# A fused top-k attention and SwiGLU kernel: three turns instead of four from top-k to V, and top-k scratch inside the penalty's buffer

## Chip, core and metric

The kernel runs on one core of a Trainium2 chip. The metric is device time in microseconds (us) of one execution, as the median of the timed runs. All data is FP32.

## What is computed

Attention over 8 batches, 8 heads, 576 tokens, head dimension 64, in which only the 32 largest scores of a row take part; then a SwiGLU block over the 4608 tokens. Cut to what matters:

```python
scores = q @ k.T / sqrt(64)                      # 8 x 8 x 576 x 576
kth    = partition(scores, -32)[..., -32]         # the 32nd largest of a row
scores = where(scores >= kth, scores, -1e9)
attn   = softmax(scores)                          # sum + 1e-9 below
x      = (attn @ v) -> (4608, 512)                # heads side by side
g      = x @ w_gate                               # 512 x 1536
out    = (g * sigmoid(g) * (x @ w_val)) @ w_out   # 1536 x 512
```

## The kernel before

**Units and turns.** The attention is cut into 160 units. A unit is 128 query rows of two heads; each batch has four query tiles (`qt` 0 to 3) by four head pairs, and a fifth tile (`qt == J`, 64 rows) in which the two heads share the 128 partitions, so that its unit has the vector work of one head only. These are called long and short units here. A batch is 16 long units and then 4 short ones.

The main loop makes one turn for each unit `n`. A unit takes part in several turns, each time in another step:

- `scores(n)` (one turn ahead): matmuls into PSUM (L294, L308), copied by ScalarE to a tile `sc` (L299, L313).
- `select(n)`: VectorE finds the 32nd largest value in four rounds of MAX8 (L329), between them MATCH_REPLACE8 (L333), which writes the scores without the eight found. It writes them to a scratch tile `rest`, one buffer. A TENSOR_SCALAR (L339) then writes the penalty, a very negative number where a score is too small and zero elsewhere, to a tile `e`, four buffers.
- `penalize(n)`: GpSimd adds the scores to `e` (L351), and prepares the bias of the softmax (L349).
- `weigh(n)`: ScalarE takes the exponential of `e` in place and sums the rows (L360, L365).
- `normalize(n)`: VectorE takes the reciprocal of the sums (L372), ScalarE multiplies `e` by it (L375).
- `turn(n)`: TensorE transposes `e` into PSUM (`etps`, L387), ScalarE copies it to `et` (L388).
- `values(n)`: TensorE multiplies by V (`av`, L407 and L416), ScalarE copies the result into `xT` (L431), the input of the SwiGLU block.

**Feed-forward blocks.** Every 256 tokens of `xT` are a block. There are 18. A block becomes available when `values` has run for the last unit that touches it. `feed(kb)` yields pieces: 24 gate and value pieces (L471) of one credit each, and then, for all blocks but the first, seven quarter products (L557) of 1.5 credits each. One credit is 8 matmul records of 128x256 in the trace (each matmul leaves two records). The weights are rounded during the first turns by all engines (L106 to L123).

**Order.** The engines run in the order in which the program issues, since a dependency between neighbours is added at the end. So the order inside a turn is the order on every engine's queue. A turn issues, in this sequence: the feed-forward leftovers of ScalarE (`flush(on_act)`); `penalize(n-1)`; the leftovers of GpSimd; `turn(n-3)`; `values(n-4)`; the score matmuls of `n+1`; a weight-rounding step of ScalarE (`early`); `weigh(n-1)`; the score copies of `n+1`; two of seven steps of top-k of `n`; up to two feed-forward pieces; two more steps of top-k; `normalize(n-2)`; transposes of the next K and Q (`fetch`) where they are due; the rest of top-k of `n` and of the pieces.

How many pieces a turn issues comes from `share(n)`: `6.4` credits for a long unit (`7.0` until the last weight tables exist), half of that for a short one, less the attention work of that turn on TensorE. For the last four units every turn issues up to 8.

```python
for m, cost in ((n + 1, 0.7), (n - TURN, 0.6), (n - VALUES, 0.7)):
    if m >= 0:
        others += cost * (0.5 if units[m][1] == J else 1)
```

**Buffers.** PSUM has five banks shared by transposes, scores and values, and three for the feed-forward. In SBUF `sc` has two buffers, `rest` one, `e` four, `et` two.

Of the kernel before, what the change touches and what calls it, by code (L numbers as in the profile page):

```python
# [10 lines left out]
FP32 = mybir.dt.float32  # L11
# [4 lines left out]
P = 128  # L16
TOP_K = 32
LOWEST = -3.4028234663852886e38
# [7 lines left out]
def kernel(  # L26
# [38 lines left out]
    B, H, S, D = q.shape  # L65
# [16 lines left out]
    work = ctx.enter_context(tc.tile_pool(name="work", bufs=2))  # L82
# [118 lines left out]
    def rounding(n):  # L201
        for _ in range(n):
            next(weight, None)
# [70 lines left out]
    def n_heads(qt):  # L274

        return 1 if qt == J else 2

    def scores(n):
        b, qt, hp = units[n]
        slab = preps[b * NHP + hp]  # L280
        sc = work.tile([P, 2 * S], FP32, tag="sc", name="sc", bufs=2)
        halves = [slice(0, D), slice(D, P)]
        half = S // 2

        def bank():
            return ps_t.tile([P, 512], FP32, tag="t", name="s")


        if qt == J:
            banks = [bank() for _ in range(2)]  # L290
            for i, ps in enumerate(banks):
                for d in halves:
                    k0 = R + i * half
                    nc.tensor.matmul(  # L294
                        ps[d, 0:half], slab[d, S + R : S + 2 * R], slab[d, k0 : k0 + half]
                    )
            yield
            for i, ps in enumerate(banks):
                nc.scalar.copy(sc[:, i * half : (i + 1) * half], ps[:, 0:half])  # L299
        else:  # L300
            q0 = S + 2 * R + qt * P
            banks = []
            for i in range(2):
                for hh, d in enumerate(halves):
                    ps = bank()
                    banks.append((i + 2 * hh, ps))
                    k0 = (1 - hh) * R + i * half
                    nc.tensor.matmul(  # L308
                        ps[:, 0:half], slab[d, q0 : q0 + P], slab[d, k0 : k0 + half]
                    )  # L310
            yield
            for i, ps in banks:
                nc.scalar.copy(sc[:, i * half : (i + 1) * half], ps[:, 0:half])  # L313
        state[n] = dict(sc=sc)

    def select(n):

        nh = n_heads(units[n][1])
        sc = state[n]["sc"]
        m = small.tile([P, 2, TOP_K], FP32, tag="m", name="m", bufs=2)  # L320
        heads = [slice(t * S, (t + 1) * S) for t in range(nh)]
        rest = work.tile([P, 2 * S], FP32, tag="rest", name="rest", bufs=1)
        e = work.tile([P, 2 * S], FP32, tag="e", name="e", bufs=4)
        state[n] |= dict(m=m, e=e, heads=heads)
        cur = sc
        rounds = TOP_K // 8
        for r in range(rounds):
            for t, hs in enumerate(heads):
                nc.vector.max(m[:, t, 8 * r : 8 * r + 8], cur[:, hs])  # L329
                yield  # L330
            if r < rounds - 1:
                for t, hs in enumerate(heads):
                    nc.vector.match_replace(  # L333
                        rest[:, hs], m[:, t, 8 * r : 8 * r + 8], cur[:, hs], LOWEST
                    )
                    yield
                cur = rest
        for t, hs in enumerate(heads):
            nc.vector.tensor_scalar(  # L339
                e[:, hs], sc[:, hs], m[:, t, TOP_K - 1 : TOP_K], FAR, ALU.is_lt, ALU.mult  # L340
            )
# [26 lines left out]
    def normalize(n):  # L368
        st = state[n]
        tot, e, heads = st.pop("tot"), st["e"], st.pop("heads")  # L370
        nh = len(heads)
        nc.vector.reciprocal(tot[:, 0:nh], tot[:, 0:nh])  # L372
        yield
        for t, hs in enumerate(heads):
            nc.scalar.mul(e[:, hs], e[:, hs], tot[:, t : t + 1])  # L375

    def turn(n):

        last = units[n][1] == J
        e = state[n].pop("e")  # L380
        et = work.tile([P, 2 * J + 1, P], FP32, tag="et", name="et")
        for c0, cn in ((0, J), (J, 1)) if last else ((0, J), (J, 1), (J + 1, J)):
            ps = ps_t.tile([P, 512], FP32, tag="t", name="etps")
            kl = R if last and c0 == J else P
            for c in range(cn):
                k0 = (c0 + c) * P
                nc.tensor.transpose(ps[0:kl, c * P : (c + 1) * P], e[:, k0 : k0 + kl], ident[:])  # L387
            nc.scalar.copy(  # L388
                et[0:kl, c0 : c0 + cn, :],
                ps[0:kl, 0 : cn * P].rearrange("p (c j) -> p c j", c=cn),  # L390
            )
            if c0 == J:
                yield
        state[n]["et"] = et
# [58 lines left out]
    def flush(queue):  # L453
        while queue:
            queue.pop(0)()
# [201 lines left out]
    NU = len(units)  # L657
# [3 lines left out]
    def piece():  # L661

        if len(on_act) > 1:
            flush(on_act)
        if len(on_pool) > 1:
            flush(on_pool)
        while True:
            if not current:
                if not todo or done.get(todo[0], 0) < NHP * BLK:
                    return 0  # L670
                flush(on_act)
                flush(on_pool)
                current.append(feed(todo.pop(0)))
            cost = next(current[0], 0)
            if cost == 0:
                current.pop()
                continue
            return cost

    def fetch(n):  # L680

        b, qt, hp = units[n]
        i = b * NHP + hp
        if qt == 0:
            yield from prep(i)
        if qt == J and i + NHP < len(pairs):
            load(i + NHP)

    def share(n):


        others = 0.0
# [3 lines that stand above are left out]
        if units[n + 2][1] == 0:  # L696
            others += 0.6

        beside = 6.4 if T[1] else 7.0
        return beside * n_heads(units[n][1]) / 2 - others  # L700

    def pieces(n):
        for _ in range(n):
            if credit[0] >= 1:
                credit[0] -= piece()

    def run(steps):
        for _ in steps:
            pass

    def finish_unit(n):
        values(n)
        b, qt, hp = units[n]
        if qt == J and b + 1 < B:
            load_v((b + 1) * NHP + hp)
# [3 lines left out]
    load(1)  # L719
    run(fetch(0))  # L720
    run(scores(0))
    early[0]()
    run(fetch(1))
    credit = [0.0]
    no = iter(())
    over = {}
    TURN, VALUES = 3, 4
    due = [2.0]
    for n in range(NU + VALUES):
        nh = n_heads(units[n][1]) if n < NU else 1  # L730
        topk = select(n) if n < NU else no
        over[n - 1] = normalize(n - 1) if 0 <= n - 1 < NU else no
        nxt = scores(n + 1) if n + 1 < NU else no
        ahead = fetch(n + 2) if n + 2 < NU else no
        norm = over.pop(n - 2, no)

        def dve(k, beside=True):

            for _ in range(k * nh):
                next(topk, None)  # L740
                due[0] += 5 / 6 if beside else 0
                if due[0] >= 1:
                    due[0] -= 1
                    rounding(1)

        if n >= NU - NHP:
            credit[0] = 8.0
        else:
            credit[0] = min(credit[0] + share(n), share(n) + 1)
        flush(on_act)  # L750
        if 0 <= n - 1 < NU:
            penalize(n - 1)
        flush(on_pool)
        if 0 <= n - TURN < NU:
            run(turn(n - TURN))
        if n >= VALUES:
            finish_unit(n - VALUES)
        next(nxt, None)

        early[0]()  # L760
        if 0 <= n - 1 < NU:
            weigh(n - 1)
        run(nxt)


        dve(2, beside=False)
        if 2 <= n + 2 < NHP:
            load(n + 2)
        if n < NHP:
            load_v(n)  # L770
        pieces(2)
        flush(on_act)
        dve(1)
        dve(1)
        next(norm, None)
        run(norm)

        flush(on_pool)
        next(ahead, None)
        pieces(1)  # L780
        next(ahead, None)
        dve(1)
        pieces(1)
        dve(2, beside=False)
        run(topk)
        pieces(6)
    while piece():
        pass
# [48 lines left out]
```

## Time and profile before

| what | us |
|---|---|
| median of 3 timed runs | 1821.04 (1820.66 to 1822.96) |
| span of the profiled execution | 1817.8 |
| what the median has over the span | 3.2 |
| TensorE busy | 1708.7 |
| VectorE busy | 1610.7 |
| ScalarE busy | 1218.7 |
| GpSimd busy | 1036.4 |

The page gives the profiled execution's span and no other time of its own. Busy time is time in which an engine executes; for TensorE matmuls overlap, so that its busy share says when it had work, not how well it was used. A row of the timeline gives start and duration in us, the engine, the line, the operation, the tiles as output<-inputs, how many instructions were merged, and in brackets how long the engine was idle before, with what released it. The span is also shown as 40 slices of 45.4 us with a digit for the busy tenths of each engine, and with the clock that TensorE was granted.

### The profile page before, as it was taken

The page shows a single profiled execution, that of the slowest core. Times are in us where ns is not written, and L with a number is a line of the kernel's source. Part 1 is how long each engine was busy: PE and PEld are TensorE (multiplying, and loading weights), DVE is VectorE, ACT ScalarE, POOL GpSimd, SP SyncE. Part 2 cuts the span into 40 slices and gives each one's busy share as a digit, 9 for nine tenths or more (in the row PEclk, how much of TensorE's full clock was granted, in tenths as well). Part 3 has the DMA queues.
Part 4 walks back from the last instruction along what each step waited for, and adds up shares of the span by engine and source line. Part 5 has one row for each costly group of instructions (what it writes and reads, how often), then busy time and mean ns, then how long its engine had stood idle before and what let it go on. Part 6 is the DMA issues. An engine that isn't in the chain of part 4 may idle for free.

```text
span 1817.8 us, 30526 instructions
## 1 busy us (share of the span) xinstructions
PE 1708.7 (94%) x10756; PEld 1409.2 (78%) x10756; DVE 1610.7 (89%) x3372; ACT 1218.7 (67%) x2977; POOL 1036.4 (57%) x930
## 2 busy tenths in 40 slices
PE   4458999899999899999999999999999999999999
PEld 2346778687788788887888878887888878888887
DVE  7999999999999799997999989998999989998400
ACT  6778666676667676666767676767676766675532
POOL 5788756455565645554455636564556554646354
PEclk6669999899999999999999999999999999999999
DMA  7432030002100030000300021000300011000000
GB/s 191 125 108 90 14 85 7 12 1 50 45 1 13 2 82 12 13 1 22 73 12 2 13 56 39 1 12 3 74 19 13 1 36 33 1 13 12 1 12 12
DMA packets 109305, 59.65 MB, mean 33 GB/s; under 512 B 88544, under 2 KB 96992, under 8 KB 109152
## 3 DMA queue, kind: packets, MB, share of 16 engines
q1 hardware_dynamic: 108016, 57.37, 12.1%
q8 instruction: 85, 1.39, 0.3%
q14 instruction: 68, 0.56, 0.1%
q10 hardware_dynamic: 1136, 0.33, 0.1%
HBM read 48.23 MB, written 9.44 MB: 32 GB/s over the span
## 4 chain that ended last, share of the span: by engine, by line
PE 86%; DVE 8%; ACT 2%; POOL 2%; issue 2%; DMA 0%; SPq 0%; ACTq 0%; POOLq 0%
PE f L471 41%; PE x_ps L557 9%; PE av L416 8%; PE etps L387 7%; PE s L308 7%; PE y_ps L557 7%; DVE m L329 3%; DVE rest L333 3%; PE s L294 2%; PE av L407 1%; PE o_ps L517 1%; PE kqps L263 1%; DVE size L121 1%; DVE e L339 0%; POOL p L543 0%
## 5 line engine op out<-in xcount | busy, mean ns | idle before, releaser
L329 DVE MAX8 m<-rest 128x8 f32<-128x576 f32 x864 | 612.7, 744 | 2.2
L351 POOL TENSOR_TENSOR e<-e,sc 128x1152 f32<-128x1152 f32 (+1 forms) x160 | 383.1, 2394 | 83.7 <-DVE e L339 76.3
L333 DVE MATCH_REPLACE8 rest<-m,rest 128x576 f32<-128x576 f32 x576 | 423.1, 740 | 0.0
L471 PE MATMUL f<-xT,wg 128*128 128x256 f32 x1728 | 401.6, 382 | 0.0
L471 PE MATMUL f<-xT,wv 128*128 128x256 f32 x1728 | 399.1, 382 | 0.0
L471 PEld LDWEIGHTS f<-xT,wg 128*128 128x128 f32 x1728 | 323.1, 190 | 62.6 <-issue 21.3
L471 PEld LDWEIGHTS f<-xT,wv 128*128 128x128 f32 x1728 | 324.5, 190 | 58.7 <-issue 16.6
L499 POOL TENSOR_TENSOR h<-h,half_g 128x512 f32<-128x512 f32 x108 | 138.2, 1280 | 292.7 <-ACT h L498 292.2
L329 DVE MAX8 m<-sc 128x8 f32<-128x576 f32 x288 | 205.0, 747 | 104.0 <-ACT sc L299 57.8
L388 ACT COPY et<-etps 128x512 f32<-128x512 f32 (+1 forms) x448 | 184.1, 483 | 131.0 <-PE etps L387 130.2
L360 ACT ACTIVATE e<-e,bias 128x576 f32<-128x576 f32 x288 | 222.1, 777 | 57.5 <-POOL e L351 57.2
L387 PE MATMUL etps<-ident,e 128*128 128x128 f32 (+1 forms) x1312 | 184.5, 286 | 79.3 <-POOL size L122 18.2
L504 POOL TENSOR_TENSOR h<-h,val 128x512 f32<-128x512 f32 x108 | 139.6, 1293 | 186.3 <-ACT val L503 186.1
L387 PEld LDWEIGHTS etps<-ident,e 128*128 128x128 f32 (+1 forms) x1312 | 159.6, 147 | 106.0 <-POOL size L122 20.7
L375 ACT ACTIVATE e<-e,tot 128x576 f32<-128x576 f32 x288 | 212.0, 790 | 0.9 <-DVE tot L372 0.9
L333 DVE MATCH_REPLACE8 rest<-m,sc 128x576 f32<-128x576 f32 x288 | 211.5, 740 | 0.0
L308 PE MATMUL s<-kqT 64*128 64x288 f32 x1024 | 178.8, 449 | 14.1 <-ACT kqT L268 8.3
L339 DVE TENSOR_SCALAR e<-sc,m 128x576 f32<-128x576 f32 x288 | 177.2, 651 | 3.4
L416 PE MATMUL av<-et,v 128*64 128x128 f32 (+1 forms) x2560 | 170.3, 278 | 0.0
L313 ACT COPY sc<-s 128x288 f32<-128x288 f32 x512 | 164.0, 402 | 2.9 <-PE s L308 2.9
L496 ACT ACTIVATE h<-f 128x512 f32<-128x512 f32 x108 | 65.2, 604 | 133.3 <-PE f L471 133.3
L416 PEld LDWEIGHTS av<-et,v 128*64 128x64 f32 x2560 | 134.1, 143 | 22.8 <-issue 6.8
(73 smaller groups left out, 2029.1 us busy)
## 6 DMA issues: line engine op xcount, KB each, us to landing
v<-in_v_dram SPq DMA_DIRECT2D x32, 256.0 KB, 2.9
kq_in<-in_k_dram SPq DMA_DIRECT2D x63, 128.0 KB, 2.8
kq_in<-in_q_dram SPq DMA_DIRECT2D x63, 128.0 KB, 3.0
w<-in_moe_w_gate_dram SPq DMA_DIRECT2D x12, 512.0 KB, 3.7
w<-in_moe_w_val_dram SPq DMA_DIRECT2D x12, 512.0 KB, 3.8
w<-in_moe_w_out_dram SPq DMA_DIRECT2D x12, 512.0 KB, 3.5
out_dram<-o SPq DMA_DIRECT2D x38, 128.0 KB, 2.4
out_dram<-o SPq DMA_DIRECT2D x16, 256.0 KB, 2.4
```

What stands on the lines that cost most here:

```text
L308: nc.tensor.matmul(ps[:, 0:half], slab[d, q0 : q0 + P], slab[d, k0 : k0 + half])
L329: nc.vector.max(m[:, t, 8 * r : 8 * r + 8], cur[:, hs])
L333: nc.vector.match_replace(rest[:, hs], m[:, t, 8 * r : 8 * r + 8], cur[:, hs], LOWEST)
L339: nc.vector.tensor_scalar(e[:, hs], sc[:, hs], m[:, t, TOP_K - 1 : TOP_K], FAR, ALU.is_lt, ALU.mult)
L351: nc.gpsimd.tensor_tensor(e[:, every], e[:, every], sc[:, every], ALU.add)
L360: nc.scalar.activation(e[:, hs], e[:, hs], AF.Exp, bias=bias[:, t : t + 1], scale=scale, accum_out=tot[:, t : t + 1],)
L375: nc.scalar.mul(e[:, hs], e[:, hs], tot[:, t : t + 1])
L387: nc.tensor.transpose(ps[0:kl, c * P : (c + 1) * P], e[:, k0 : k0 + kl], ident[:])
L388: nc.scalar.copy(et[0:kl, c0 : c0 + cn, :], ps[0:kl, 0 : cn * P].rearrange("p (c j) -> p c j", c=cn),)
L416: nc.tensor.matmul(av[hh * R : (hh + 1) * R, 0:ql], v_last[:, hh, :] if c == J else vt[:, hh, c, :], moving, start=last and c == 0, stop=c ...
L471: nc.tensor.matmul(ps[:, i, :], w[:, kc, m * P : (m + 1) * P], x[:, kc, :], start=(kc == 0), stop=(kc == KC - 1),)
L557: nc.tensor.matmul(ps, lhsT, T[i][m], start=m == 0, stop=m == MQ - 1)
```

## The change

The step after top-k is shortened by one turn. `normalize(n-1)` has its reciprocal at the end of turn `n`, behind all of top-k, and its two multiplications at the start of turn `n+1`, ahead of `values` and the scores. `turn` comes in the middle of a turn, for the unit two back, where normalization was. `values` is for the unit three back. The score copies are issued right after the score matmuls, ahead of `weigh`. MATCH_REPLACE8 writes to `e`, which the penalty overwrites later, so that `rest` is gone; `e` has three buffers and `sc` three.

```diff
     def scores(n):
...
-        sc = work.tile([P, 2 * S], FP32, tag="sc", name="sc", bufs=2)
+        sc = work.tile([P, 2 * S], FP32, tag="sc", name="sc", bufs=3)
...
     def select(n):
...
-        rest = work.tile([P, 2 * S], FP32, tag="rest", name="rest", bufs=1)
-        e = work.tile([P, 2 * S], FP32, tag="e", name="e", bufs=4)
+        e = work.tile([P, 2 * S], FP32, tag="e", name="e", bufs=3)
...
                     nc.vector.match_replace(
-                        rest[:, hs], m[:, t, 8 * r : 8 * r + 8], cur[:, hs], LOWEST
+                        e[:, hs], m[:, t, 8 * r : 8 * r + 8], cur[:, hs], LOWEST
                     )
                     yield
-                cur = rest
+                cur = e
...
-    over = {}
-    TURN, VALUES = 3, 4
+    scaled = no
+    TURN, VALUES = 2, 3
...
     for n in range(NU + VALUES):
...
-        over[n - 1] = normalize(n - 1) if 0 <= n - 1 < NU else no
+        norm = normalize(n - 1) if 0 <= n - 1 < NU else no
...
-        norm = over.pop(n - 2, no)
...
         if 0 <= n - 1 < NU:
             penalize(n - 1)
         flush(on_pool)
-        if 0 <= n - TURN < NU:
-            run(turn(n - TURN))
+        run(scaled)
         if n >= VALUES:
             finish_unit(n - VALUES)
-        next(nxt, None)
-
+        run(nxt)
         early[0]()
         if 0 <= n - 1 < NU:
             weigh(n - 1)
-        run(nxt)
...
         flush(on_act)
         dve(1)
         dve(1)
-        next(norm, None)
-        run(norm)
+        if 0 <= n - TURN < NU:
+            run(turn(n - TURN))
...
         run(topk)
+        next(norm, None)
+        scaled = norm
         pieces(6)
```

## The prediction

> **What bounds the kernel now.** I read the 40 slices first, to see which engine is full where; then TensorE's timeline at the start; then TensorE's waits; then the timeline of the end. The slices:
>
> ```profile
> PE   4458999899999899999999999999999999999999
> DVE  7999999999999799997999989998999989998400
> PEclk6669999899999999999999999999999999999999
> ```
>
> VectorE is full from the first slices and done before the last two. TensorE is half idle in three and a half slices, at a reduced clock, and full to the end. So this is VectorE-bound for some 150 us and TensorE-bound after it. Only removing TensorE idle time shortens the span. All of it is 1817.8 - 1708.7 = 109 us; a table of 40 us windows puts 77 of that before 160 us, 8.2 in the window 320 to 360, the rest in crumbs of 1 to 5. The start, in TensorE's timeline:
>
> ```profile
> 130.80 2.15 PE L387 MATMUL etps<-ident,e 128*128 128x128 f32 x9 [4.84 <-POOL size L122]
> ...
> 143.61 2.15 PE L387 MATMUL etps<-ident,e 128*128 128x128 f32 x9 [7.08 <-POOL wo L123]
> ...
> 149.20 1.39 PE L308 MATMUL s<-kqT 64*128 64x288 f32 x6 [0.56 <-ACT et L388]
> 150.52 3.72 PE L471 MATMUL f<-xT,wg 128*128 128x256 f32 x16
> 154.08 3.62 PE L471 MATMUL f<-xT,wv 128*128 128x256 f32 x16
> 157.53 3.62 PE L471 MATMUL f<-xT,wg 128*128 128x256 f32 x16
> 160.98 1.15 PE L387 MATMUL etps<-ident,e 128*128 128x128 f32 x9
> ```
>
> The transposes open a turn. Turn 10 starts at 130.80, turn 11 at 143.61. Turn 10 ends in 7.08 us of nothing; in turn 11 the first block is available (units 0 to 7, the last at `values(n-4)`), and the 48 records, six credits, run to the next turn: 10.46 us, 1.74 a credit. The waits of TensorE from 160 to 1700 us (total, times, longest):
>
> ```profile
> PE etps L387 <- issue: 12.4, 8, 3.6
> PE etps L387 <- ACT e L375: 9.9, 7, 4.6
> ```
>
> Of these 22.3 us, 8.2 lie at 338 to 356, where blocks 0 and 1 are used up and block 2 isn't there until turn 31 (its first matmul is at 361.11): three turns of attention alone. The other 14 are at short units. VectorE's own waits there (`m` for `sc`, 72 us from 160 to 1675) cost nothing while TensorE is full. The end:
>
> ```profile
> 1746.53 2.75 PE L557 MATMUL x_ps<-wo,h 128*128 128x256 f32 x12
> ...
> 1751.69 0.77 PE L387 MATMUL etps<-ident,e 128*128 128x128 f32 x5 [0.99 <-ACT e L375]
> ...
> 1754.14 3.72 PE L471 MATMUL f<-xT,wg 128*128 128x256 f32 x16
> ```
>
> Block 16 ends at 1749.3, the last block starts at 1754.1 and fills TensorE to the end; only 1 us there is idle.
>
> **What the skill says.** "Perfetto Trace Analysis", Optimization Strategy: where the most contended engine changes over time, interleaving the regimes may help. The slices show just two such regimes. "TensorE: Matmul & The Clock Gate", What's actually happening: after idling the array runs at half clock until it has been busy for a few us; the nine transposes take 2.15 us at the start and 1.15 at 160.98, which agrees. "SBUF — State Buffer", Who interferes with whom: a TENSOR_SCALAR in a two-port mode and GpSimd block each other, an instruction with one SBUF input outside these modes doesn't. L339 has a median of 510 ns and a maximum of 2035, MAX8 727 to 762, which fits. So a changed phase between the two engines moves only L339.
>
> **The change part by part.**
>
> Scratch in `e`: 864 MATCH_REPLACE8 stay at 740 ns, and the SBUF is 4.6 KB a partition smaller. New is a wait: the first MATCH_REPLACE8 of unit n must wait for the transposes of n-3, in the middle of turn n-1. A TensorE-bound turn lasts 11.37 us (transposes at 321.60 and 332.97); in it the transposes would follow 1.5 us of `av`, 1.2 of scores and two pieces, 3.5, and end at 7.4. VectorE begins a turn 6.6 us or more after TensorE began the turn before (802.51 to 809.08), and its first replacement 1.4 later, at 8.0. It just misses the wait. Behind it would stand all of top-k, and GpSimd's L351 after that; bounds: 0 to 1 us of VectorE a turn, none of it on the path where TensorE is full. I take 0.
>
> Score copies ahead of `weigh`: four copies of 0.4 us no longer stand behind L351 (2.4 us) and two exponentials. VectorE's wait for `sc` should shrink. But the reciprocal at the end of top-k of n now waits for `weigh(n-1)`, and the next top-k is queued behind it. That is the same chain (L339, L351, L360, L365), less the copies (1.28 us) and plus, on ScalarE, the multiplications (1.5 us) that run while GpSimd adds. VectorE's lead stays within about 1 us of what it was: 0.
>
> The reciprocal itself leaves the middle of the next top-k, half a turn earlier: a gain where TensorE waited for the multiplications behind it (12.4 us of "issue", of which 4.8 outside the hungry turns). What is late next is `et`: `av` at the head of turn n+1 needs copies that stand on ScalarE behind `weigh` and the gate functions, as the multiplications did before. So most of the 7.9 us of the second row stays. Bounds for all crumbs: 14 us gained to 17 lost (34 waits of L360 for L351 by half a us each). I take 2 gained.
>
> `values` a turn earlier: block 0 starts in turn 10. Its six credits fall into the 7.08 us that were idle, and everything after follows a turn earlier. All 36 weight pieces get two steps each, five steps a turn: by turn 10 some 54 steps, 25 pieces ready; the block wants 24 within five turns. Nothing to wait for. While VectorE sets the pace, up to turn 30, this changes no turn's time. At the hungry turns block 2 starts in turn 30 (347.4) instead of 31 (356.1); the hunger is as long as before. From there the lead is one long turn's pieces: 6.4 - 0.7 - 0.6 - 0.7 = 4.4 credits, 4.4 x 1.74 = **7.6 us** of TensorE work done in idle time, which the tail no longer has. V's loads on SP are issued a turn earlier, from turn 19, in a queue that is then nearly empty: 0. DVE may lose up to 1 us in turn 10, by L339 beside more GpSimd work: 0 to 2, I take 0.5.
>
> The end: block 16 now ends inside turn 159, and the last unit's chain lies open: the last copy of the block 0.6, multiplication 0.8, `xT` copy 0.2, exponential with sums 1.3, reciprocal 0.2, multiplication 0.8, transposes 0.7, copy 0.7, `av` 1.0: 6.3 us against the 4.9 seen, so 1.4 lost (0, if ScalarE is ahead, to 4, if GpSimd's L351 is late).
>
> Sum: -7.6 - 2 + 0.5 + 1.4 = -7.7. Span 1810; with the 3.2 us that the median has over the span, **1813**.
>
> **The rivals.** Main case, the lead carried to the end: 0.56; its own range is 1808 to 1818.
> *More*: looser coupling also removes the 14 us of crumbs. For it: reciprocal and copies both come earlier. Against: `et` takes the multiplications' place. 1821 - 7.6 + 0.9 + 1.4 - 12 = 1804, chance 0.16.
> *Nothing*: the lead is given back, since blocks come as they are used up and the last chain is open, or waits on `e` and `et` keep V as late as it was. The price is 4 us at the end and 3 in hungry turns: 1820, chance 0.14.
> *Slower*: `av` at the head of a turn waits for `et`. With the numbers above, the copies end at 9 to 10 us of 11.4 when L351 is on time; in the turn from 624.63 the exponential came at 632.01, 7.4 us in, and with 2.1 for it, 1.8 for gate functions and 1.2 for the copies they end at 12.6, 1.2 too late. If the 34 turns in which L360 waits for L351 cost 0.5 us each, that is 17 us: 1830. It decides from 0.23 us a turn on (7.7 / 34). For it: GpSimd is 57% busy and in order. Against: transposes had the same queue ahead of them before. 0.14.
>
> **How the numbers follow.** About 0.2%, 3.6 us, is what a measurement can tell here. Faster takes the whole of "more" and nearly all of the main case: 0.70. Same takes "nothing" and the main case's edge: 0.16; slower 0.14. The range, 1803 to 1823, leaves out the slower case and some of "more".
>
> **What would show it.** Right: the first L471 near 138, a turn of 12 us before 150.5; the first of block 2 near 350; the last block's start 4 to 8 us before 1754; idle time of TensorE before 160 us about 8 lower; the clock up one slice earlier. VectorE's waits for `sc` should shrink, with waits of L372 for L365 in their place, and few for L387. Wrong: a row of `av` waiting for L388 of over 8 us, or a first L471 at 138 with the last block no earlier.

## The result and the profile after

The changed kernel takes **1809.38 us** (median of 4 runs, 1809.13 to 1810.53) against 1820.98 for the kernel before (4 runs on the same chip). The ratio is 0.9936, with a 95% interval of 0.9922 to 0.995: 11.6 us faster, where 8 were forecast. The profiled execution took 1810.53 us with a span of 1808.5. The spans differ by 9.3 us. The other 2.3 come from the two executions that were profiled. In the 67 runs of the kernel before beside the experiments, the time is 1.7 to 1.9 us longer than the span, and 2.0 in those of the change. So the 3.2 us by which the median before exceeds its profiled span mean that this execution was some 1.4 us shorter than usual; the one after was 1.1 us longer than its median.

Line numbers of the changed kernel are lower by one from the top-k on: L470 is a gate or value matmul, L386 a transpose, L387 the `et` copy, L406 and L415 are `av`. The slices of its page:

```profile
PE   4559999799999999999999999999999999999999
DVE  7999999999999999998999989998999979999400
PEclk7559999999999999999999999999999999999989
```

TensorE gains in the second and fourth slice, and it has a 7 instead of an 8 in the eighth, where the hungry turns are (turns for which no feed-forward block is available). New is the 8 in its clock in the last slice but one. TensorE's timeline at the start, and at block 2:

```profile
130.91 0.80 PE L406 MATMUL av<-et,vlast 128*128 128x128 f32 x2 [3.12 <-ACT et L387]
...
135.66 3.75 PE L470 MATMUL f<-xT,wg 128*128 128x256 f32 x16
139.25 1.15 PE L386 MATMUL etps<-ident,e 128*128 128x128 f32 x9
...
147.14 0.38 PE L406 MATMUL av<-et,vlast 128*128 128x128 f32 x2
...
347.44 1.56 PE L470 MATMUL f<-xT,wg 128*128 128x256 f32 x6
```

The first gate records stand at 135.66 instead of 150.52, and the transposes now come between them. Block 2 begins at 347.44 instead of 361.11. TensorE's idle time before 160 us fell from 77.5 to 66.7. But there is a wait that was not there before, in brackets in the first row: `av` waits for `et`. TensorE's waits from 160 to 1700 us (total, times, longest):

```profile
PE av L406 <- ACT et L387: 17.6, 19, 2.7
PE av L415 <- ACT et L387: 3.2, 5, 0.6
```

and VectorE's over the whole run:

```profile
DVE tot L371 <- ACT tot L364: 79.7, 32, 14.4
...
DVE e L332 <- PE etps L386: 25.2, 29, 2.3
DVE m L328 <- ACT sc L313: 9.3, 1, 9.3
```

The waits of MAX8 for `sc` (57.8 us for L299 and 46.1 for L313 before) have all but gone, and the reciprocal waits for the sums instead. MATCH_REPLACE8 does wait for the transposes that free its buffer. The end, in the timeline of all engines:

```profile
1730.41 2.75 PE L556 MATMUL x_ps<-wo,h 128*128 128x256 f32 x12
...
1733.92 1.27 POOL L542 TENSOR_TENSOR o<-o,p 128x512 f32<-128x512 f32 x1 [1.83 <-ACT o L645]
1735.33 1.40 POOL L350 TENSOR_TENSOR e<-e,sc 128x576 f32<-128x576 f32 x1
1736.76 0.78 ACT L359 ACTIVATE e<-e,bias 128x576 f32<-128x576 f32 x1 [2.20 <-POOL e L350]
...
1743.20 5.38 PE L470 MATMUL f<-xT,wg 128*128 128x256 f32 x16
```

Block 16 ends at 1733.2, 16 us earlier than before, but the last block starts only 10.9 us earlier. Between the two lie 10.0 us instead of 4.9: GpSimd adds the last unit's scores (L350) after block 16's last sum (L542), and everything of that unit follows. TensorE idles in it, and the first 16 records of the last block then take 5.38 us instead of 3.72.

**A balance.** TensorE runs in the program's order, so its time can be cut at the first score record of units 20, 140 and 159. "Rest" is the time of a stretch less 0.2158 us for each feed-forward record in it (16 records at full speed stand 3.45 us apart; a record of block 0's output counts as two). It holds attention, waits, and what a lower clock costs; the last column ends with TensorE's last record. All numbers are worked out from one trace of each kernel; "six batches" is units 20 to 139, split into the five units that open a batch, the ten long ones after them, and the last five, of which four are short. Three pairs of kernels that hardly differ (before and the scratch of experiment 1; the change and seven credits; V late with three `et` buffers and with two) agree within 1.4 us until unit 20 and within 0.8 in six batches.

| kernel | unit 20 at, with records done | rest of six batches: opening / long / short | sum | rest, last batch | rest after unit 159 |
|---|---|---|---|---|---|
| before | 235.4, 248 | 113.2 / 230.7 / 129.0 | 472.9 | 74.3 | 10.1 |
| after | 233.9, 288 | 117.0 / 228.3 / 127.4 | 472.8 | 70.0 | 15.5 |
| copies first (four turns) | 235.2, 248 | 112.5 / 233.9 / 131.6 | 478.0 | 73.0 | 10.1 |
| normalize first only | 239.1, 248 | 124.2 / 253.3 / 122.5 | 500.0 | 77.2 | 9.1 |
| copies behind, V late | 235.2, 248 | 121.1 / 246.8 / 116.6 | 484.5 | 71.8 | 9.6 |
| V late | 229.8, 248 | 111.1 / 233.3 / 112.2 | 456.6 | 70.7 | 9.6 |
| V late, two `et` | 231.2, 248 | 111.1 / 232.5 / 112.2 | 455.8 | 70.7 | 9.6 |
| transposes at head | 238.2, 288 | 116.6 / 243.9 / 113.6 | 474.1 | 72.7 | 13.3 |
| transposes before gates | 236.3, 288 | 124.0 / 230.0 / 126.8 | 480.8 | 71.5 | 17.6 |
| V in mid-turn | 235.5, 288 | 120.3 / 239.4 / 123.3 | 483.0 | 72.3 | 18.0 |
| seven credits | 233.7, 288 | 117.0 / 228.3 / 127.5 | 472.8 | 70.0 | 9.0 |
| transposes by kind | 234.1, 288 | 117.0 / 228.3 / 111.8 | 457.1 | 69.7 | 8.9 |

From before to after: 1.5 us less until unit 20, which is hardly more than two traces differ by, and 40 records more done by then (8.6 us), together -10.1; nothing in six batches; -4.4 in the last batch; +5.4 after unit 159. That is the 9.3 us, within rounding. The experiments ask what the nothing in six batches is made of, and whether the rest of the sum is what I took it for.

### The profile page after: what moved, and what is told of

The parts are those of the page before. It is cut to its first block, busy times and chain, and to the rows that moved or that the text cites. A ratio compares the mean times of both kernels' runs of the same rounds, so it can differ in the third digit from the quotient of the medians.

```text
span 1808.5 us, 30379 instructions
## 1 busy us (share of the span) xinstructions
PE 1703.6 (94%) x10756; PEld 1402.5 (78%) x10756; DVE 1615.7 (89%) x3372; ACT 1221.0 (68%) x2977; POOL 1039.2 (57%) x930
## 3 DMA queue, kind: packets, MB, share of 16 engines
q8 instruction: 85, 1.39, 0.3%
## 4 chain that ended last, share of the span: by engine, by line
PE 83%; DVE 8%; ACT 6%; POOL 2%; issue 0%; DMA 0%; SPq 0%; ACTq 0%; POOLq 0%
PE f L470 40%; PE x_ps L556 9%; PE av L415 8%; PE s L308 7%; PE y_ps L556 7%; PE etps L386 6%; DVE m L328 3%; DVE e L332 3%; PE s L294 2%; PE av L406 2%; ACT et L387 1%; PE o_ps L516 1%; ACT e L359 1%; DVE e L338 1%; DVE size L121 1%; ACT kqT L268 1%
## 5 line engine op out<-in xcount | busy, mean ns | idle before, releaser
L328 DVE MAX8 m<-e 128x8 f32<-128x576 f32 x864 | 614.1, 746 | 3.3
L350 POOL TENSOR_TENSOR e<-e,sc 128x1152 f32<-128x1152 f32 (+1 forms) x160 | 383.0, 2394 | 86.1 <-DVE tot L371 70.1
L332 DVE MATCH_REPLACE8 e<-m,e 128x576 f32<-128x576 f32 x576 | 423.1, 740 | 0.0
L470 PE MATMUL f<-xT,wg 128*128 128x256 f32 x1728 | 406.5, 383 | 0.6 <-ACT xT L430 0.6
L470 PE MATMUL f<-xT,wv 128*128 128x256 f32 x1728 | 403.4, 382 | 0.0
L470 PEld LDWEIGHTS f<-xT,wg 128*128 128x128 f32 x1728 | 321.6, 191 | 61.0 <-issue 19.8
L470 PEld LDWEIGHTS f<-xT,wv 128*128 128x128 f32 x1728 | 320.6, 190 | 59.3 <-issue 19.7
L387 ACT COPY et<-etps 128x512 f32<-128x512 f32 (+1 forms) x448 | 182.4, 480 | 53.6 <-PE etps L386 52.8
L332 DVE MATCH_REPLACE8 e<-m,sc 128x576 f32<-128x576 f32 x288 | 211.5, 739 | 0.0
L386 PE MATMUL etps<-ident,e 128*128 128x128 f32 (+1 forms) x1312 | 175.9, 279 | 18.7 <-ACT xT L430 12.7
L386 PEld LDWEIGHTS etps<-ident,e 128*128 128x128 f32 (+1 forms) x1312 | 155.9, 144 | 42.7 <-issue 25.2
L313 ACT COPY sc<-s 128x288 f32<-128x288 f32 x512 | 167.6, 417 | 26.5 <-PE s L308 25.3
L308 PE MATMUL s<-kqT 64*128 64x288 f32 x1024 | 170.3, 454 | 15.9 <-ACT kqT L268 15.1
L415 PE MATMUL av<-et,v 128*64 128x128 f32 (+1 forms) x2560 | 173.6, 280 | 6.9 <-ACT et L387 6.9
L415 PEld LDWEIGHTS av<-et,v 128*64 128x64 f32 x2560 | 136.4, 144 | 32.1 <-ACT et L387 9.3
```

What stands on the lines that cost most here:

```text
L308: nc.tensor.matmul(ps[:, 0:half], slab[d, q0 : q0 + P], slab[d, k0 : k0 + half])
L332: nc.vector.match_replace(e[:, hs], m[:, t, 8 * r : 8 * r + 8], cur[:, hs], LOWEST)
L350: nc.gpsimd.tensor_tensor(e[:, every], e[:, every], sc[:, every], ALU.add)
L387: nc.scalar.copy(et[0:kl, c0 : c0 + cn, :], ps[0:kl, 0 : cn * P].rearrange("p (c j) -> p c j", c=cn),)
L415: nc.tensor.matmul(av[hh * R : (hh + 1) * R, 0:ql], v_last[:, hh, :] if c == J else vt[:, hh, c, :], moving, start=last and c == 0, stop=c ...
L470: nc.tensor.matmul(ps[:, i, :], w[:, kc, m * P : (m + 1) * P], x[:, kc, :], start=(kc == 0), stop=(kc == KC - 1),)
```

## The experiments

Each kernel ran beside the kernel before; the ratio is to that, with its 95% interval.

**1. Scratch in `e`, alone and taken back.** Alone, in the kernel before:

```diff
-        rest = work.tile([P, 2 * S], FP32, tag="rest", name="rest", bufs=1)
...
-                        rest[:, hs], m[:, t, 8 * r : 8 * r + 8], cur[:, hs], LOWEST
+                        e[:, hs], m[:, t, 8 * r : 8 * r + 8], cur[:, hs], LOWEST
...
-                cur = rest
+                cur = e
```

> The kernel before with one part: MATCH_REPLACE8 writes to e (four buffers kept), rest is gone. The prediction took 0 for it: 1820 to 1822 us, MATCH_REPLACE8 at 740 ns. Rival: a MATCH_REPLACE8 that waits for transposes of an older unit costs VectorE time in the VectorE-bound start and lengthens the span, over 1823.

Measured: 1820.95 us, 1.0003 (0.9995 to 1.0012). Taken back in the changed kernel (a separate `rest`, `e` still with three buffers):

> The changed kernel with MATCH_REPLACE8 writing to a tile of its own again (one buffer), e with three and sc with three buffers. VectorE's waits of MATCH_REPLACE8 for transposes (25 us in 29 waits) go. The prediction's value for this wait was 0, since VectorE has slack where TensorE is full: 1807.5 to 1811. Rival (VectorE's lead is what TensorE lives on at short units, so the waits are on the path): 1795 to 1805.

Measured: 1808.94 us, 0.9936 (0.9924 to 0.9949), the ratio of the change itself. The 25.2 us of waits at MATCH_REPLACE8 are gone from its profile, and VectorE's waits at the reciprocal have grown from 79.7 to 98.9 us instead. Most of the waiting has moved elsewhere. The scratch costs nothing that can be measured here, as forecast.

**2. The score copies ahead of `weigh`, in four turns.** The kernel of experiment 1 (scratch in `e`, four buffers), with three `sc` buffers and:

```diff
-        next(nxt, None)
-
+        run(nxt)
         early[0]()
         if 0 <= n - 1 < NU:
             weigh(n - 1)
-        run(nxt)
```

> The kernel before, with MATCH_REPLACE8 writing to e (four buffers kept), three buffers of sc, and the score copies issued ahead of weigh; normalization in mid-turn, transposes at the head, four turns, as before. In the changed kernel TensorE reaches the scores of unit 159 at 1706.3 us instead of 1714.1, 7.8 us earlier, beside the feed-forward lead. Theory A (the early score copies free VectorE from GpSimd and ScalarE): these 7.8 us appear here too, 1812 to 1816 us, and the waits of m for sc (104 us before) nearly vanish. Theory B (the reciprocal at the end of top-k, ahead of a turn instead of inside it, does it): VectorE's waits shrink, but TensorE gains nothing, 1819.5 to 1822.5.

Measured: 1825.16 us, 1.0022 (1.0014 to 1.003). Both theories missed. VectorE's waits for `sc` fell only from 104 to 89 us, and TensorE's rest rose by 5 in six batches. In the old order this part loses. The third `sc` buffer and the new place of the copies come together here; no run has them apart.

**3. Normalization at the head of a turn, with the old order behind it.** The changed kernel, four `e` buffers, and:

```diff
-    TURN, VALUES = 2, 3
+    TURN, VALUES = 3, 4
...
         run(scaled)
+        if 0 <= n - TURN < NU:
+            run(turn(n - TURN))
...
         dve(1)
-        if 0 <= n - TURN < NU:
-            run(turn(n - TURN))
```

> The changed kernel with transposes for unit n-3 back at the head of the turn, values four units back, e with four buffers; normalization first, score copies first and scratch in e stay. It stands beside the version with values four units back (1793.9 us), from which it differs only in where the transposes stand. Theory H1 (the gain of that version comes from transposes in mid-turn: TensorE has V, scores and two pieces to do before it needs e, and runs ahead in the VectorE-bound start): 1814 to 1821. Theory H2 (it comes from the reciprocal ahead of the turn instead of inside it, so that nothing waits for the multiplications): 1791 to 1800, and no waits of etps after 400 us.

Measured: 1853.68 us, 1.0186 (1.0172 to 1.02), slower than both theories. That is 59 us more than V late with two `et` buffers (1794.93, experiment 5), which has its transposes in mid-turn instead of at the head of the next turn, and three `e` buffers, and differs in nothing else. The first row of TensorE's waits after 160 us:

```profile
PE s L308 <- ACT et L387: 27.7, 26, 6.0
```

The scores wait for `et` copies, which they don't read. Scores, transposes and `av` share five PSUM banks, and a bank that transposes filled comes free with its copy. On ScalarE that copy now stands behind the two multiplications (1.5 us). A long turn asks for eight banks in the order three for transposes, one for `av`, four for scores. If the five are given in turn, the second, third and fourth of the score matmuls take the banks of the same turn's transposes. The idle time fits that: in the first 15 units of each of the six batches, 177 ns on average stand ahead of the second score matmul and 70 ahead of the third, none ahead of the first. The wait shown is the smaller part. Idle time after 160 us is 38.3 us instead of 31.5, but TensorE's busy time rose from 1708.7 to 1734.7 us for the same 10756 matmul records.

**4. The other half of that pair.** The changed kernel with V a turn later, three `et` buffers, and the score copies behind `weigh` as before:

```diff
-    TURN, VALUES = 2, 3
+    TURN, VALUES = 2, 4
...
-        run(nxt)
+        next(nxt, None)
         early[0]()
         if 0 <= n - 1 < NU:
             weigh(n - 1)
+        run(nxt)
```

> The version with values four units back (1793.9 us), with the score copies behind weigh again as in the kernel before. Theory (the copies ahead of weigh give VectorE its scores without GpSimd; since VectorE now waits at its reciprocal for the same weigh, they matter little): 1793 to 1797. Rival (the copies ahead are worth what VectorE waited for sc before, some of it on the path): 1800 to 1812.

Measured: 1826.14 us, 1.003 (1.0019 to 1.0041), 32 us slower than the same kernel with the copies ahead (experiment 5) and beyond what the rival gave it. TensorE's waits after 160 us:

```profile
PE etps L386 <- ACT sc L313: 26.2, 15, 4.2
```

The transposes don't read `sc`; what they can need of a score copy is the bank that it frees. So with transposes in mid-turn the copies have to stand ahead of `weigh`. Experiments 2 to 4 together: copies first, without the other two parts, +5 us; with normalization moved too, but not the transposes, +33; both moved, but not the copies, +6. The parts gain only together. The rows of waits point to the order in which ScalarE frees PSUM banks as what couples them; no run with another number of banks tests that.

**5. V as late as before.** The changed kernel with `values` four back and three `et` buffers:

```diff
-        et = work.tile([P, 2 * J + 1, P], FP32, tag="et", name="et")
+        et = work.tile([P, 2 * J + 1, P], FP32, tag="et", name="et", bufs=3)
...
-    TURN, VALUES = 2, 3
+    TURN, VALUES = 2, 4
```

> The changed kernel with values again four units back (et gets a third buffer), all else as changed: blocks become available a turn later. Theory: of the 11.6 us gained, the feed-forward lead (4.4 credits, 7.6 us) is lost, and the open chain ahead of the last block (10.0 us from the end of block 16 to the first matmul of block 17, 4.9 before; 1.7 more at a reduced clock) is covered again: 1809.4 + 7.6 - 6.9, so 1808 to 1813. Rival 1 (the lead is all of the gain): 1819 to 1822. Rival 2 (the chain stays open a turn later): 1815 to 1818.

Measured: **1793.91 us**, 0.9855 (0.9838 to 0.9871). No theory had that: 15.5 us faster than the change, though blocks start a turn later again (first gate record at 145.40) and 248 records are done at unit 20 instead of 288. It reaches unit 20 at 229.8, 4.1 us sooner than the change, so that the early V is ahead there by 4.5 us and not by the whole 8.6. The rest of six batches is 16.2 lower, and nearly all of that lies at the short units (127.4 to 112.2). A pair of short turns in TensorE's timeline of the change, then one of this kernel:

```profile
838.43 1.15 PE L386 MATMUL etps<-ident,e 128*128 128x128 f32 x9
840.93 0.49 PE L406 MATMUL av<-et,vlast 128*128 128x128 f32 x2 [1.35 <-ACT et L387]
```

```profile
834.80 1.15 PE L386 MATMUL etps<-ident,e 128*128 128x128 f32 x9
835.78 0.39 PE L406 MATMUL av<-et,vlast 128*128 128x128 f32 x2
837.12 1.19 PE L294 MATMUL s<-kqT 64*64 64x288 f32 x8
```

In the change, `av` follows right behind the transposes whose copies it needs, and TensorE stands still. Here it reads copies of the turn before and starts at once. From scores to scores the same work (16 gate or value records, nine transposes, `av`) takes 8.67 us in the change (833.76 to 842.43) and 7.00 here (830.12 to 837.12). The third buffer isn't needed:

```diff
-    TURN, VALUES = 2, 3
+    TURN, VALUES = 2, 4
```

> The changed kernel with one number changed: VALUES is 4 instead of 3; et keeps its two buffers. The version with three buffers took 1793.9 us. Theory (what counts is the half turn between the copies to et and av; a unit's et is written in the middle of turn n, after av of the unit two before has read that buffer at its head): 1793 to 1797. Rival (the third buffer is needed, the copies to et wait for av): 1799 to 1808.

Measured: 1794.93 us, 0.9855 (0.9841 to 0.987). So the later V alone does it. Unit 20 comes at 231.2 here, and the early V is ahead by 5.9 us.

**6. What `et` stands behind.** Three ways to have `et` earlier with V kept early. First, the transposes ahead of the mid-turn gate functions of ScalarE:

```diff
         pieces(2)
+        if 0 <= n - TURN < NU:
+            run(turn(n - TURN))
         flush(on_act)
         dve(1)
         dve(1)
-        if 0 <= n - TURN < NU:
-            run(turn(n - TURN))
```

> The changed kernel with the transposes of unit n-2 and their copies issued ahead of the mid-turn flush of ScalarE's leftovers, so that the copies to et no longer stand behind gate functions (1.8 us a gate); the order on TensorE and VectorE stays. Theory (values three units back makes av wait for et at the head of the next turn, 17 us in rows of av after 160 us, and this is what the version with values four units back gets rid of): these waits fall by half or more, 1799 to 1806 us. Rival (the waits come from TensorE's own transposes or from the exponential, or cost nothing, and the version with values four units back gains by the order of blocks alone): 1808 to 1811.

Measured: 1820.96 us, 0.9999 (0.9991 to 1.0007): the whole gain lost, half of it at the openings of batches (117.0 to 124.0), and the short units hardly better (126.8). TensorE's waits of `av` at these short units fell only from 10.5 us in 13 cases to 8.0 in 12, so gate functions ahead of the copies aren't the main cause of them. A short turn without any shows what is left:

```profile
847.27 1.15 PE L386 MATMUL etps<-ident,e 128*128 128x128 f32 x9
848.60 0.29 ACT L364 ACTIVATE tot<-tot,eps 128x1 f32<-128x1 f32 x1
848.80 1.22 ACT L387 COPY et<-etps 128x512 f32<-128x512 f32 x3
849.59 0.49 PE L406 MATMUL av<-et,vlast 128*128 128x128 f32 x2 [1.18 <-ACT et L387]
```

The copies follow the last step of `weigh` and take 1.22 us, and TensorE has nothing else to do meanwhile. ScalarE's waits for transposes rose from 52.8 us in 57 cases to 137.9 in 110: the gate functions now stand behind copies that wait for TensorE. Second, the transposes right behind the scores, ahead of `weigh`:

```diff
         run(nxt)
+        if 0 <= n - TURN < NU:
+            run(turn(n - TURN))
         early[0]()
...
         dve(1)
-        if 0 <= n - TURN < NU:
-            run(turn(n - TURN))
```

> The changed kernel with the transposes of n-2 and their copies issued right behind the scores, ahead of weigh on ScalarE; values stays three units back. Outside the feed-forward records, TensorE's time from the scores of unit 20 to those of unit 140 is 473 us in the changed kernel and 457 with values four units back, nearly all of the difference in the short units. Theory (the copies to et stand behind weigh, and av at the head of the next turn waits for them; in a short turn nothing is left to cover that): the short units lose their waits and the lead of a turn stays, 1790 to 1801 us. Rival (transposes now come before TensorE has feed-forward pieces to do, so that they wait for the multiplications at the head): the waits move from av to etps, 1808 to 1825.

Measured: 1817.67 us, 0.9979 (0.997 to 0.9989). Theory and rival were both there: the short units fell to 113.6, with hardly a wait of `av` left, but the long ones rose from 228.3 to 243.9. TensorE's waits after 160 us:

```profile
PE etps L386 <- ACT xT L430: 15.5, 19, 2.6
...
PE av L406 <- ACT et L387: 0.6, 1, 0.6
```

The pieces that stood ahead of the transposes, and covered the multiplications and `xT` copies on ScalarE, now come after them. Third, `values` moved to mid-turn, just ahead of the transposes:

```diff
-        if n >= VALUES:
-            finish_unit(n - VALUES)
...
         dve(1)
+        if n >= VALUES:
+            finish_unit(n - VALUES)
         if 0 <= n - TURN < NU:
```

> The changed kernel with values(n-3) moved from the head to the middle of the turn, just ahead of the transposes of n-2: av gets half a turn of slack for et, and a block still becomes available a turn earlier than with values four units back. Theory (the waits of av for et cost 16 us from unit 20 to 140 and part of the 5.4 us at the end, the lead is worth 4.5 us against the version with values four units back): 1789 to 1797. Rival (what is gained from values four units back is the time of the blocks, not the wait of av; or the banks of PSUM, taken in another order, bring a wait of their own): 1800 to 1812.

Measured: 1827.39 us, 1.004 (1.0028 to 1.0053). The waits of `av` are gone but for 3.8 us at the end; scores now wait for `kqT` and `xT` copies (25.5 and 16.7 us over the whole run), long units cost 239.4, and TensorE is busy 1734.9 us with the same matmul records. That the order of banks is behind it fits experiments 3 and 4, but no run here isolates it.

**7. The last turns.** The change with seven credits instead of eight in the last four turns and the drain:

```diff
         if n >= NU - NHP:
-            credit[0] = 8.0
+            credit[0] = 7.0
```

> The changed kernel with 7 credits instead of 8 in each of the last four turns and the drain, so that some four pieces of block 16 are left for the turns in which the last unit runs through softmax, transposes and V. Theory (an open chain of 5.2 us and a cold clock of 1.7 us were paid there): 1803 to 1806, block 17 starts 4 to 6 us earlier. Rival (the last unit itself comes later by what is left out, or the chain hangs on GpSimd's last sums whatever is issued): 1808 to 1811.

Measured: 1802.95 us, 0.9906 (0.9891 to 0.9921). The rest after unit 159 falls from 15.5 to 9.0, and the last block starts at 1738.13. With eight credits block 16 is used up while the last unit still has its chain to go; with seven, two credits of it (16 records: 704 to 688 in the last batch, 384 to 400 behind it) are kept to cover that chain.

**8. The parts that gained, together.** V early, the transposes at the head only in the turns that select a short unit and in the drain, seven credits:

```diff
         run(nxt)
+        at_head = n >= NU or units[n][1] == J
+        if at_head and 0 <= n - TURN < NU:
+            run(turn(n - TURN))
...
-        if 0 <= n - TURN < NU:
+        if not at_head and 0 <= n - TURN < NU:
```

> The changed kernel (values a turn early kept), with the transposes and et copies at the head of the turn, behind the scores and ahead of weigh, only where the unit in selection is a short one or the stream is draining; in the turns of long units they stay mid-turn; and 7 credits instead of 8 at the last four turns. Theory (the changed kernel's short turns wait for et copies that stand behind weigh and the gates, its long turns do not, and its tail is 6 us of two extra pieces): the short turns lose some 14 us of rest over six batches (127.4 to 113), the tail 6, the lead stays, long units stay at 228: 1785 to 1796 us. Rival (what decides is the order in which PSUM banks are asked for over several turns; switching the place twice a batch has long and short turns wait for each other's banks): 1798 to 1812 us, with the long units' rest above 233 or the batch starts above 121.

Measured: **1788.09 us**, 0.9821 (0.9807 to 0.9834), the fastest of all. Its terms are those of the parts: short units 111.8, long ones unchanged at 228.3, 8.9 after unit 159, 288 records at unit 20. A short turn in ScalarE's timeline, then the same turn and the start of the last block in TensorE's:

```profile
830.76 1.24 ACT L387 COPY et<-etps 128x512 f32<-128x512 f32 x3 [0.18 <-PE etps L386]
831.87 0.80 ACT L359 ACTIVATE e<-e,bias 128x576 f32<-128x576 f32 x1
```

```profile
830.07 1.20 PE L386 MATMUL etps<-ident,e 128*128 128x128 f32 x9
831.10 3.62 PE L470 MATMUL f<-xT,wg 128*128 128x256 f32 x16
834.56 0.38 PE L406 MATMUL av<-et,vlast 128*128 128x128 f32 x2
...
1721.56 0.69 PE L415 MATMUL av<-et,v 128*64 128x64 f32 x16 [0.57 <-ACT et L387]
...
1722.44 3.72 PE L470 MATMUL f<-xT,wg 128*128 128x256 f32 x16
```

The copies now stand ahead of `weigh`, and 16 gate records cover them. Against V late with two `et` buffers, 40 more records are done at unit 20 (8.6 us) which comes 2.9 us later, six batches cost 1.3 more, and the two last stretches 1.7 less: 6.1 us less by the balance, 6.8 by the medians.

## Why the prediction came out as it did

The forecast, 1813 with a main case of 1808 to 1818, holds the 1809.4 measured, and its leading term is part of what happened. That the sum came this near is in part luck: terms that it left at or near nothing came out large and cancelled.

**The lead: there, but not alone.** Forecast 7.6 us; measured at unit 20: 40 records more (8.6 us), reached 1.5 us sooner, 10.1 in all. The first block did start in turn 10, with its first record at 135.66 where I put it near 138, and block 2 at 347.44, the time worked out for turn 30. But V late, whose blocks start as late as those of before, also reaches unit 20 sooner than before, by 4.2 to 5.6 us with the same 248 records (231.2 and 229.8 instead of 235.4). So about half of the 10.1 comes from the new order of the other stages while VectorE sets the pace, where I took 0. The early V adds 4.5 to 5.9 to that (experiment 5), and 5.7 in experiment 8: less than forecast. Which part of the order helps at the start is open; experiments 2 to 4 have none of the gain (235.2, 239.1, 235.2). The idle time before 160 us fell by 10.8, not 8, but with V late it falls by 6.9 to 7.9 too (69.6 and 70.6 us instead of 77.5), so that this sign of being right couldn't tell the two apart. The clock did not come up a slice earlier.

**The crumbs: right in sum, wrong in parts.** I took -2; it came to about nothing in six batches and -4.4 in the last one. The step that failed is the bracket "14 us gained to 17 lost", in which I treated *more* and *slower* as two cases of which one would hold. Both came true at once, and that they cancel is luck.

With V late (experiment 5) the new order of normalization, score copies and transposes is worth 17.1 us over six batches (472.9 to 455.8), 16.8 of it at the short units: that is *more*, and larger than the 12 I gave it. There 9.9 us are idle time that went (11.9 to 2.0); the rest lies inside busy time.

With V early, 17.0 is given back (455.8 to 472.8), 15.2 of it at the short units. There 10.5 us are rows of `av` waiting for `et`, and the rest shows as no wait. With the transposes moved ahead of `weigh` there, `av` waits no more at these units and they fall to 113.6 and 111.8 (experiments 6 and 8): that is the wait of *slower*. That its price was 17 too is chance, since it was worked out for other turns, those where `weigh` waits for GpSimd; half of the wait sits in short turns. The sign that I named as proof of the wrong case, a row of `av` waiting over 8 us, was there with 20.8 us, and the kernel was faster all the same; 6.1 of these lie in the hungry turns.

What the copies stand behind differs from turn to turn. ScalarE's timeline of the change, up to the `av` at 840.93:

```profile
836.94 0.30 ACT L364 ACTIVATE tot<-tot,eps 128x2 f32<-128x2 f32 x1
838.63 0.60 ACT L495 ACTIVATE h<-f 128x512 f32<-128x512 f32 x1 [1.39 <-PE f L470]
839.13 0.59 ACT L496 ACTIVATE half_g<-f 128x512 f32<-128x512 f32 x1
839.60 0.63 ACT L497 ACTIVATE h<-h 128x512 f32<-128x512 f32 x1
840.12 1.24 ACT L387 COPY et<-etps 128x512 f32<-128x512 f32 x3
```

`weigh` was done at 837.2. Then ScalarE waits 1.39 us for the gate matmuls, takes 1.5 for their functions, and only then copies `et`. Where no gate function stands there, the end of `weigh` and the copies' own time are enough (experiment 6). In a long turn TensorE has further pieces between the transposes and the next `av`; in a short one there is next to nothing.

The -4.4 of the last batch is not settled. It is there with V late too (70.7), so it isn't the early V. At the openings of batches the change is 3.8 us worse than before and 5.9 worse than with V late; experiment 8 leaves that as it is (117.0), so it isn't the place of the transposes in short turns. The trace shows 5.2 us of idle time at these openings instead of 1.5: the scores waiting for `kqT`, the copies of transposed K and Q (2.6), and `av` for `et` (2.6). In experiment 8 it is 5.6, all of it for `kqT`. Why the early V brings that wait stays open.

One reading of the prediction was off: of the 12.4 us of "issue" 6.2, not 4.8, lie outside the hungry turns (347.41 and 356.07). It doesn't change a bound that mattered.

**The end, undersized.** Forecast +1.4, within 0 to 4; measured +5.4. I summed a chain that starts with "the last copy of the block" and left GpSimd's L350 to the upper bound. It was late: it stands behind block 16's last sum (1733.92 and 1735.33). Also left out was the clock: after the idle time the first 16 records take 1.66 us more. "TensorE: Matmul & The Clock Gate" of the Trainium skill, under What's actually happening, has that: the array falls back to half clock after idling. The trace agrees, with a granted clock of 0.50 from 1739 to 1745. I had quoted it for the start alone. Experiment 7 shows that the whole term (15.5 to 9.0, where before had 10.1) hangs on the number of pieces that are kept for the last turns.

**Costed at nothing, and nothing.** Scratch in `e`: 0 by experiment 1, though the wait that "just misses" didn't miss. It was there 29 times, 25.2 us in all and so inside the bound of 1 us a turn on average, and moved VectorE's slack from one place to another. The score copies: waits for `sc` gone and waits for the sums in their place, as said. But "0" for this part was luck: in the old order it costs 5 us (experiment 2), and it is needed by the new place of the transposes (experiment 4), for a reason the prediction did not see, to which the waits point: the PSUM banks.

## What to carry to other kernels

Pulling a consumer one step nearer to its producer buys lead once, at the start (4.5 to 5.9 us here), but costs a wait in every step that is too short to cover the producer's queue. So price it per kind of step: here the long turns bore it, the short ones gave back 15 us, and a different place for the short ones alone kept both gains. And measure the lead with that one step undone, since a new order of the other stages can gain at the same place. When stages share a pool of buffers, list who frees each buffer and what stands ahead of the freeing instruction on its engine before moving any stage. And when a kernel is shortened at its head, check the tail again: the work that covered the last chain may now be used up before it.

## What was not expected of the hardware

TensorE's busy time is no constant of the work: with the same 10756 matmul records it was 1690.3 us with the transposes at the head (experiment 6), 1708.7 before, and 1734.7 and 1734.9 in experiment 3 and with V in mid-turn. Waits for PSUM banks may thus lie inside busy time, where the table of waits doesn't show them; whether these 26 us are waits at all, the runs don't separate. "Perfetto Trace Analysis" of the Trainium skill, under Identifying the Most-Contended Engine, calls the matmul busy share no good measure of how near a kernel is to its best, and takes the FLOPs done, against the peak, and the busy share of weight loads instead. The traces agree: the time of the loads stayed between 1398 and 1419 us in all these kernels, and their share of the span fell from 78% in the fastest kernel (span 1786.0) to 77% with V in mid-turn (1825.2). The matmuls' share was 95% in both.
